# Fixing the issue order of SyncE and GpSimd and moving the bulk weight loads to the GpSimd queue, in a fused attention and mixer kernel

## The chip, the core and the metric

The kernel runs on one core of one Trainium2 chip. Its time is the device time of one execution in microseconds (us). Before the change the median of three runs was 1606.46 us (1606.43 to 1606.93).

The engines are called TensorE (PE in the profile; PEld are its weight loads), VectorE (DVE), ScalarE (ACT), GpSimd (POOL) and SyncE (SP). Sixteen DMA engines serve all DMA queues of the core. A DMA issued from SyncE goes to queue q1, which the profile calls hardware_dynamic; one issued from GpSimd goes to q0, software_dynamic.

## The reference, cut to what matters

```python
def reference(x, mem0, Wq, Wk, Wv, Wo, seg_len, _, w1, w2, w3, w4):    # S=2048, D=1024, H=32, Dh=128, F=3584
    xn = layernorm(x)
    return x + A(xn) + B(xn)

def A(xn):            # segments of 32 tokens, each behind 8 memory rows carried on from the segment before
    for s in range(64):
        h = concat([mem, xn[s*32:(s+1)*32]])
        q, k, v = h@Wq, h@Wk, h@Wv                  # 32 heads of 128
        p = softmax(mask(q @ k.T * scale))
        o = (p @ v) @ Wo
        mem, out[s] = o[:8], o[8:]

def B(xn):
    h  = gelu(layernorm(xn) @ w1)
    x1 = xn + shift_channels(h) @ w2                # four channel groups, shifted along S by 1, -1, 2, -2
    return x1 + gelu(layernorm(x1) @ w3) @ w4
```

Inputs and outputs are bf16. The kernel works through it in these stages, whose names are used below:

- **first phase**: layernorms of x, the transposed tile `xn2T`, `@ w1`, gelu;
- **second phase**: `@ w2` on the shifted channels, residual, layernorm, the transposed result `xn3T`;
- **MLP**: `@ w3`, gelu (`h3T`), `@ w4`. Small units for the memory rows are mixed in, each with a 1 MB tile of Wv or Wo (`wt`, `wot`);
- **V phase**: V = xn @ Wv, written to DRAM;
- **attention**: five blocks of tokens, each with eight head groups of four heads. A head group projects Q and K from `hTb`, the block's transposed tokens (64 matmuls of 396 columns, 403 in the first block; 128 matmuls in the last), and between those projections come scores (`psS`), softmax on VectorE and ScalarE (its result is `Pn`), a DMA transpose of `Pn` into `PT` (a DMA that transposes the tile as it copies it), and the output matmuls (`psO`) that read `PT` and `V`. After a block, `pso` multiplies its outputs by Wo.

One head group reads 1 MB of Wq, 1 MB of Wk and 0.4 MB of V. Each of its four score tiles needs one small transpose `Pn` to `PT`.

## The kernel before

TensorE alone was in a hand-written order (`manual_schedule`); the other engines' orders came from a scheduler. This is the part of the attention that matters. Cuts are marked.

```python
with tc.manual_schedule(engines={mybir.EngineType.PE}), ExitStack() as actx:
    wpool = actx.enter_context(tc.tile_pool(name="aw", bufs=4, side="right"))   # 4 weight tiles of 1 MB
    # ... first phase, second phase, MLP, V phase cut ...
    def load_values(B, V, hg):
        nc.sync.dma_start(V[0:96, 0:4, :], V_d[r:r + 384, cs_].rearrange("(t p) c -> p t c", p=96))
        # ... the memory rows of V, on nc.sync too; cut ...
    def scores(t, hg, QT, KTt):
        # ... 4 psS matmuls; mask, exp, sums, reciprocal on VectorE and ScalarE; cut ...
        nc.vector.tensor_tensor(Pn[:T, :, :T], e[:T, :, :T], rs[...], op=ALU.mult)   # ring of 3 Pn
        PT = smp.tile([P, 4, 112], BF16, tag="PT", bufs=5)
        nc.sync.dma_start_transpose(PTr, Pn[:rows].rearrange("p h k -> p (h k)"))
        return PTr

    def tick(us, blocked=None):          # a nominal clock: which scores (S) or outputs (O) go out now
        clock[0] += us
        while True:
            for i, (due, kind, fn) in enumerate(smalls):
                if due <= clock[0] and kind != blocked:
                    smalls.pop(i)
                    clock[0] += fn()
                    break
            else:
                return
    LAT = 8.0                            # outputs come due 8 us after their scores
    for gi_, group in enumerate(groups):
        for hg in range(8):
            wq, wk = wtile(), wtile()
            nc.sync.dma_start(wq[:], Wq_v[:, :, cs_])
            nc.sync.dma_start(wk[:], Wk_v[:, :, cs_])
            for B, V in zip(Bs, Vs):
                load_values(B, V, hg)
            if gi_ == 0 and hg < 4:
                nc.sync.dma_start(wo_sb[:, hg * 8:(hg + 1) * 8, :], Wo_v[:, hg * 8:(hg + 1) * 8, :])
            for w, dsts, scale in ((wq, QTs, QSCALE), (wk, KTs, None)):
                for hh in range(4):
                    proj(B, w, hh, dst, scale)
                    tick(...)
            # ... queue this head group's scores, due evenly over the next head group; cut ...
```

In the first phase four of 16 tiles of `xn2T` were transposed on TensorE, the others by DMA transposes on SyncE. `w2` (2 MB) was loaded after the third group. The second phase loaded `xn` and transposed `xn3T` on SyncE, tile by tile; `w3` (seven chunks of 1 MB) came behind it in the text, on SyncE too.

Of the kernel before, what the change touches and what calls it, by code (L numbers as in the profile page):

```python
# [23 lines left out]
P = 128  # L24
# [53 lines left out]
def kernel(  # L78
# [107 lines left out]
    with tc.manual_schedule(engines={mybir.EngineType.PE}), ExitStack() as actx:  # L186
# [5 lines left out]
        with ExitStack() as bctx:  # L192
            psum = bctx.enter_context(tc.tile_pool(name="psum", bufs=2, space=PSUM))
            with ExitStack() as hctx:
# [4 lines left out]
                nc.gpsimd.memset(hTB[:, :, 0:2], 0.0)  # L199
                nc.gpsimd.memset(hTB[:, :, S + 2:S + 4], 0.0)  # L200

                with ExitStack() as p0:
# [3 lines left out]
                    xts = [ring.tile([P, D], BF16, tag="xt", bufs=8, name=f"xt{n}") for n in range(NT)]  # L206

                    def load_x(n):
                        nc.sync.dma_start(xts[n][:], x_v[:, n, :])
# [5 lines left out]
                    for n in range(3, 8):  # L215
                        load_x(n)

                    def norm(n, xn2T, jj, on_pe):
                        xt = xts[n]
                        st = ring.tile([P, 2, 6], F32, tag="st")  # L220
                        for c in range(2):
                            nc.vector.bn_stats(st[:, c, :], xt[:, c * 512:(c + 1) * 512])
                        mv = ring.tile([P, 2], F32, tag="mv")
                        nc.vector.bn_aggr(mv[:], st[:])
                        ab = ring.tile([P, 2], F32, tag="ab")
                        nc.vector.tensor_scalar(ab[:, 0:1], mv[:, 1:2], EPS, None, op0=ALU.add)
                        nc.vector.tensor_scalar(ab[:, 1:2], ab[:, 0:1], EPS, mv[:, 1:2], op0=ALU.mult, op1=ALU.add)
                        rr = ring.tile([P, 2], F32, tag="rr")
                        nc.gpsimd.tensor_tensor(rr[:], ab[:], neghalf[:], op=ALU.pow)
                        nm2 = ring.tile([P, 1], F32, tag="nm2")  # L230
                        nc.vector.tensor_scalar(nm2[:], mv[:, 0:1], rr[:, 1:2], -1.0, op0=ALU.mult, op1=ALU.mult)
                        xn2 = ring.tile([P, D], BF16, tag="xn2")
                        nc.scalar.activation(xn2[:], xt[:], ACTF.Identity, bias=nm2[:], scale=rr[:, 1:2])
                        if not on_pe:
                            nc.sync.dma_start_transpose(xn2T[:, jj], xn2[:])
                        xn = ring.tile([P, D], BF16, tag="xn")
                        nc.vector.tensor_scalar(xn[:], xt[:], mv[:, 0:1], rr[:, 0:1], op0=ALU.subtract, op1=ALU.mult)
                        nc.gpsimd.dma_start(xn_v[:, n, :], xn[:])
                        if n + 8 < NT:
                            load_x(n + 8)  # L240
                        return xn, xn2

                    def transposes(xn2, xn2T, jj):
                        for k0 in (0, 4):
                            ps = psum0.tile([P, 4, P], F32, tag="tr")
                            for k in range(4):
                                nc.tensor.matmul(ps[:, k, :], xn2[:, (k0 + k) * P:(k0 + k + 1) * P], ident[:], start=True, stop=True)
                            if k0 == 0:
                                nc.vector.tensor_copy(xn2T[:, jj, k0:k0 + 4, :], ps[:])
                            else:  # L250
                                nc.scalar.copy(xn2T[:, jj, k0:k0 + 4, :], ps[:])
# [7 lines left out]
                    def stage1(n0, nt, xn2T, between):  # L259
                        w = nt * P  # L260
                        for co in range(KT):
# [5 lines left out]
                            if between and co % 2 == 1:  # L267
                                between.pop(0)()

                    groups = []  # L270
                    n0 = 0
                    for nt in (1, 1, 2, 2, 2, 4, 4):
                        groups.append((n0, nt))
                        n0 += nt
                    todo = []
                    prev = None
                    for (n0, nt) in groups:
                        xn2T = ring.tile([P, 4, KT, P], BF16, tag="xn2T", bufs=2)
                        on_pe = n0 < 4
                        trs, sms = [], []  # L280
                        for jj in range(nt):
                            xn, xn2 = norm(n0 + jj, xn2T, jj, on_pe)
                            if on_pe:
                                trs.append(lambda xn2=xn2, jj=jj, xn2T=xn2T: transposes(xn2, xn2T, jj))
                            sms.append(lambda n=n0 + jj, xn=xn: seg_sums(n, xn))
                        if prev is None:
                            for f in trs:
                                f()
                            todo = sms
                        else:  # L290
                            todo = trs + todo
                            stage1(*prev, todo)
                            for f in todo:
                                f()
                            todo = sms
                        prev = (n0, nt, xn2T)
                        if n0 == 4:
                            nc.sync.dma_start(w2_sb[:], w2_v)
                    stage1(*prev, todo)
                    for f in todo:  # L300
                        f()

# [34 lines left out]
            with ExitStack() as p3:  # L337
# [129 lines left out]
                while pending or units:  # L467
                    spec_step()
# [384 lines left out]
```

## Time and profile before

| stage (from the first and last TensorE instruction of each, in the trace) | us |
|---|---|
| first phase | 13.4 to 96.6 |
| second phase | 96.4 to 151.8 |
| MLP | 151.7 to 587.7 |
| V phase | 587.5 to 808.7 |
| attention | 809.6 to 1599.2 |
| span | 1604.6 |

From the page of the kernel before (span 1604.6 us): TensorE's busy time, its share and its instructions; and the DMA queues with packets, megabytes and the share of the 16 engines' time.

```profile
PE 1537.0 (96%) x10222; PEld 830.5 (52%) x10222; DVE 525.3 (33%) x1149; ACT 511.5 (32%) x1183; POOL 89.7 (6%) x114
...
q1 hardware_dynamic: 333888, 249.23, 58.2%
q0 software_dynamic: 6080, 21.05, 3.5%
```

TensorE is the limit: 96% busy. Nearly all bytes go through SyncE's queue. What is left to win stands in TensorE's waits of the kernel before: who waits, for what, the sum in us, how often, and the longest.

```profile
PE ps L247 <- ACT xn_152 L233: 13.4, 1, 13.4
PE psO L575 <- DMA PT<-Pn_6360: 10.1, 9, 2.1
PE ps L264 <- DMA xn2T<-xn_788: 8.2, 1, 8.2
PE ps L370 <- DMA wt<-in_A_Wv_dram: 5.2, 2, 3.9
PE ps L436 <- ACT h3T L437: 4.8, 1, 4.8
...
PE gps_3027 L384 <- DMA wot<-in_A_Wo_dram: 3.5, 2, 3.0
...
PE psO L575 <- DMA PT<-Pn_6359: 2.6, 3, 1.2
PE psO L575 <- DMA PT<-Pn_6361: 2.5, 4, 1.5
```

The start costs 13.4 us. The three PT lines together (one for each of the three Pn buffers) cost 15.2 us in the whole attention.

One more view: what SyncE issued in one head group of the kernel before, in order (start, us, instruction).

```profile
892.09 1.19 SPq L566 DMA_TRANSPOSE PT<-Pn_6361  x1
893.86 0.40 SPq L629 DMA_DIRECT2D wt<-in_A_Wq_dram  x1
895.12 1.19 SPq L566 DMA_TRANSPOSE PT<-Pn_6359  x1
896.41 1.47 SPq L524 DMA_DIRECT2D V_7498<-V_scratch  x1
898.26 1.18 SPq L566 DMA_TRANSPOSE PT<-Pn_6360  x1
...
900.41 0.57 SPq L630 DMA_DIRECT2D wt<-in_A_Wk_dram  x1
901.24 1.23 SPq L566 DMA_TRANSPOSE PT<-Pn_6361  x1
```

### The profile page before, as it was taken

How to read it: one execution, taken by the hardware profiler on the slowest of the kernel's cores; microseconds unless marked ns; L12 is line 12 of the kernel's file. 1: busy time of each engine (PE TensorE's matmuls, PEld its weight loads, DVE VectorE, ACT ScalarE, POOL GpSimd, SP SyncE). 2: the span in 40 equal slices, each digit the busy share in tenths (PEclk: the TensorE clock that was granted, in tenths of full speed). 3: DMA queues.
4: the chain of work that ended last, by engine and by line, in shares of the span. 5: the costliest groups of instructions: out<-in, count | busy, mean ns of one | idle time of the engine just before them, and what ended most of it. 6: DMA issues, size and time to landing. Idle time of an engine off the chain costs nothing.

```text
span 1604.6 us, 25081 instructions
## 1 busy us (share of the span) xinstructions
PE 1537.0 (96%) x10222; PEld 830.5 (52%) x10222; DVE 525.3 (33%) x1149; ACT 511.5 (32%) x1183; POOL 89.7 (6%) x114
## 2 busy tenths in 40 slices
PE   5799998999999999999999999999999999999998
PEld 4544444454454444444455645654655566466654
DVE  6248000001010112212235533551554165325541
ACT  4423300301202101111146623650563266146630
POOL 4223001001011010000000000000000000000000
PEclk9899999999999999999999999999999999999999
DMA  9869525265382567433369965993798388348521
GB/s 316 242 190 298 190 86 177 79 208 186 91 243 75 109 193 266 132 105 120 105 196 254 236 155 131 245 232 89 213 233 201 108 223 228 91 128 196 115 48 48
DMA packets 340087, 271.93 MB, mean 169 GB/s; under 512 B 155987, under 2 KB 309736, under 8 KB 339968
## 3 DMA queue, kind: packets, MB, share of 16 engines
q1 hardware_dynamic: 333888, 249.23, 58.2%
q0 software_dynamic: 6080, 21.05, 3.5%
q8 instruction: 82, 1.34, 0.4%
q14 instruction: 37, 0.30, 0.1%
HBM read 191.52 MB, written 42.53 MB: 146 GB/s over the span
## 4 chain that ended last, share of the span: by engine, by line
PE 73%; DMA 9%; DVE 1%; issue 1%; ACT 0%; POOL 0%; SPq 0%; ACTq 0%; POOLq 0%
PE ps L540 23%; PE pso L593 14%; PE ps L481 14%; PE ps L436 9%; PE ps L460 8%; DMA PT<-Pn_6360 3%; PE psO L575 2%; PE psS L551 2%; DMA PT<-Pn_6361 2%; DMA PT<-Pn_6359 1%; DMA hTb<-xn_scratch 1%; PE ps L693 1%; DMA R_scratch<-R_3128 1%; PE ps L404 1%; DMA wot<-in_A_Wo_dram 1%
## 5 line engine op out<-in xcount | busy, mean ns | idle before, releaser
L540 PE MATMUL ps<-hTb,wt 128*128 128x396 bf16 (+1 forms) x2560 | 403.7, 311 | 0.0
L540 PEld LDWEIGHTS <-wt 128*128 128x128 bf16 x3072 | 272.0, 98 | 167.3 <-issue 4.5
L481 PE MATMUL ps<-wt,xT 128*128 128x512 bf16 x1024 | 221.2, 379 | 0.0
L460 PE MATMUL ps<-w_sb,h3T 128*128 128x512 bf16 x896 | 198.5, 382 | 0.0
L437 ACT ACTIVATE h3T<-ps 128x512 bf16<-128x512 f32 x112 | 66.6, 597 | 315.0 <-PE ps L436 310.6
L481 PEld LDWEIGHTS <-xT 128*128 128x128 bf16 x1024 | 100.2, 98 | 120.8
L436 PEld LDWEIGHTS <-w_sb 128*128 128x128 bf16 x896 | 88.1, 99 | 112.3 <-issue 11.4
L460 PEld LDWEIGHTS <-h3T 128*128 128x128 bf16 x896 | 87.1, 98 | 103.3 <-issue 2.7
L557 DVE TENSOR_REDUCE sums<-sm 99x4 f32<-99x396 f32 (+1 forms) x176 | 97.6, 554 | 117.6 <-ACT sm L555 117.5
L553 DVE TENSOR_TENSOR sm<-psS,c_mask_reg_sb 99x396 f32<-99x396 f32 x160 | 91.2, 570 | 109.6 <-PE psS L551 108.9
L483 ACT CAST Vs<-ps 128x512 bf16<-128x512 f32 x64 | 37.4, 586 | 230.2 <-PE ps L481 177.5
L555 ACT ACTIVATE sm<-sm 99x396 f32<-99x396 f32 (+1 forms) x176 | 92.8, 527 | 54.0 <-DVE sm L553 49.8
L485 DVE CAST Vs<-ps 128x512 bf16<-128x512 f32 x64 | 44.3, 692 | 176.5 <-PE ps L481 172.7
L540 PE MATMUL ps<-hTb_5138,wt 128*128 128x403 bf16 x512 | 93.6, 335 | 2.4 <-ACT QT_6369 L544 1.5
L264 PE MATMUL ps<-xn2T,w_sb 128*128 128x256 bf16 (+2 forms) x448 | 65.9, 309 | 13.8 <-DMA xn2T<-xn_788 8.2
L601 DVE TENSOR_TENSOR ot<-pso,Rt 128x512 bf16<-128x512 f32 x32 | 22.1, 691 | 156.1 <-PE pso L593 152.8
L264 PEld LDWEIGHTS <-w_sb 128*128 128x128 bf16 x448 | 41.0, 106 | 32.7 <-issue 9.8
L436 PE MATMUL ps<-xn3T_1209,w_sb 128*128 128x512 bf16 x224 | 51.4, 393 | 4.8 <-ACT h3T L437 4.8
L315 PE MATMUL ps<-w_sb,hTB 128*128 128x512 bf16 x256 | 55.4, 379 | 0.0
L436 PE MATMUL ps<-xn3T_1210,w_sb 128*128 128x512 bf16 x224 | 51.0, 390 | 0.0
L436 PE MATMUL ps<-xn3T_1211,w_sb 128*128 128x512 bf16 x224 | 49.0, 379 | 0.0
L436 PE MATMUL ps<-xn3T_1212,w_sb 128*128 128x512 bf16 x224 | 48.5, 379 | 0.0
(613 smaller groups left out, 1407.1 us busy)
## 6 DMA issues: line engine op xcount, KB each, us to landing
wt<-in_A_Wq_dram SPq DMA_DIRECT2D x40, 1024.0 KB
wt<-in_A_Wk_dram SPq DMA_DIRECT2D x40, 1024.0 KB
wt<-in_A_Wv_dram SPq DMA_DIRECT2D x24, 1024.0 KB
w_sb<-in_B_w_dram SPq DMA_DIRECT2D x16, 1024.0 KB
V_scratch<-Vs SPq DMA_DIRECT2D x32, 512.0 KB
wot<-in_A_Wo_dram SPq DMA_DIRECT2D x8, 1024.0 KB
wo_sb<-in_A_Wo_dram SPq DMA_DIRECT2D x4, 2048.0 KB
Rt<-R_scratch SPq DMA_DIRECT2D x32, 256.0 KB
```

Source lines behind the costliest of these rows:

```text
L264: nc.tensor.matmul(ps[:, :w].rearrange("p (n t) -> p n t", t=P), w1_sb[:, k, co * P:(co + 1) * P], xn2T[:, :nt, k, :], start=(k == 0), sto ...
L315: nc.tensor.matmul(ps[:], hTB[:, k, o:o + P], w2_sb[:, k, ch * 512:(ch + 1) * 512], start=(k == 0), stop=(k == KT - 1))
L436: nc.tensor.matmul(ps[:].rearrange("p (n t) -> p n t", t=P), w3_sb[:, k, f * P:(f + 1) * P], xn3T[tb][:, :, k, :], start=(k == 0), stop=(k ...
L437: nc.scalar.activation(h3T[:, f, :], ps[:], ACTF.Gelu_apprx_tanh)
L460: nc.tensor.matmul(ps[:], h3T[:, f, j * P:(j + 1) * P], w4_sb[:, f, ch * 512:(ch + 1) * 512], start=(f == 0), stop=(f == FT - 1))
L481: nc.tensor.matmul(ps[:], xT[:, m4 * 4 + j, k, :], wv[:, k, :], start=(k == 0), stop=(k == KT - 1))
L485: nc.vector.tensor_copy(Vs[:, j, :], ps[:])
L540: nc.tensor.matmul(ps[:, :nb] if B["b"] in (0, 5) else ps[:, :nb].rearrange("p (t c) -> p t c", t=4), w[:, k, hh * P:(hh + 1) * P], B["rhs ...
L553: nc.vector.tensor_tensor(sm[:T, :, :T], S3, t["mask"][:].unsqueeze(1).to_broadcast((T, 4, T)), op=ALU.add)
L555: nc.scalar.activation(e[:T, :, :T], sm[:T, :, :T], ACTF.Exp, scale=LN2)
L557: nc.vector.tensor_reduce(ss, e[:T, :, :T], axis=AX.X, op=ALU.add)
L593: nc.tensor.matmul(self.ps[:], self.oX[:, h, self.gl * P:(self.gl + 1) * P], wo_sb[:, h, self.cc], start=(h == 0), stop=(h == H - 1))
```

## The change

Its intent: SyncE and GpSimd get a hand-written order too. Bulk weights go to GpSimd's queue, so that SyncE's queue is left to the transposes and small loads. The first phase is software-pipelined by hand, with VectorE and ScalarE in fixed order and eight of 16 tiles transposed on TensorE. Wo is loaded in the V phase instead of in the attention. The core of the diff (cuts marked):

```diff
-    with tc.manual_schedule(engines={mybir.EngineType.PE}), ExitStack() as actx:
+    with tc.manual_schedule(engines={mybir.EngineType.PE, mybir.EngineType.SP, mybir.EngineType.Pool}), ExitStack() as actx:
 # first phase (rewritten, cut): first xn2 on VectorE, groups of (1, 1, 2, 2, ...) tiles, NPE = 8 tiles transposed on TensorE
+            def load_w3(c):
+                nc.gpsimd.dma_start(w3_sb[:, :, c * 512:(c + 1) * 512], w3_v[:, :, c * 512:(c + 1) * 512])
+                        if n0 == 8:
                             nc.sync.dma_start(w2_sb[:], w2_v)
+                        if n0 >= 8:
+                            load_w3((n0 - 8) // 2)
 # second phase, tile n: xn loaded three tiles ahead
+                        load_xn(n + 3)
+                        nc.sync.dma_start_transpose(xn3T[n // 4][:, n % 4], xn3[:])
                         nc.gpsimd.dma_start(R1_v[:, n, :], x1[:])
-                        nc.sync.dma_start_transpose(xn3T[n // 4][:, n % 4], xn3[:])
+                        if n < 3:
+                            load_w3(4 + n)
-            for c in range(7):
-                nc.sync.dma_start(w3_sb[:, :, c * 512:(c + 1) * 512], w3_v[:, :, c * 512:(c + 1) * 512])
 # MLP: Wv and Wo tiles of the memory units on nc.gpsimd, asked for one or two units ahead (cut)
 # V phase: Wo here, Wv two head groups ahead
+                if 1 <= hg < 5:
+                    nc.gpsimd.dma_start(wo_sb[:, (hg - 1) * 8:hg * 8, :], Wo_v[:, (hg - 1) * 8:hg * 8, :])
 # attention
-                nc.sync.dma_start(V[0:96, 0:4, :], V_d[r:r + 384, cs_].rearrange("(t p) c -> p t c", p=96))
+                nc.gpsimd.dma_start(V[0:96, 0:4, :], V_d[r:r + 384, cs_].rearrange("(t p) c -> p t c", p=96))
 # (the memory rows of V likewise, cut)
-                nc.sync.dma_start(wq[:], Wq_v[:, :, cs_])
-                nc.sync.dma_start(wk[:], Wk_v[:, :, cs_])
+                nc.gpsimd.dma_start(wq[:], Wq_v[:, :, cs_])
+                nc.gpsimd.dma_start(wk[:], Wk_v[:, :, cs_])
         def tick(us, blocked=None):
             clock[0] += us
-            while True:
-                for i, (due, kind, fn) in enumerate(smalls):
-                    if due <= clock[0] and kind != blocked:
-                        smalls.pop(i)
-                        clock[0] += fn()
-                        break
-                else:
-                    return
+            done = set()                                  # one S and one O per step, at most five S without their O
+            for item in list(smalls):
+                due, kind, fn = item
+                if due <= clock[0] and kind != blocked and kind[0] not in done and not (kind[0] == "S" and flying[0] >= 5):
+                    smalls.remove(item)
+                    flying[0] += 1 if kind[0] == "S" else -1
+                    done.add(kind[0])
+                    clock[0] += fn()
```

## The prediction

> **What bounds the kernel now.** TensorE: the page gives it 1537.0 us busy of a 1604.6 us span, so 67.5 us idle. The list of waits names 61 of it: start 13.4; first phase, DMA transposes 8.2 and 3.6, a PSUM copy 1.8; weight loads in the MLP (speculative Wv and Wo tiles) 5.2 and 3.5; h3T after the second phase's last transpose 4.8; in the attention phase (after 800 us) the transposed probabilities PT 15.2, oT_m copies 2.9, others 2.4. Longer gaps cost twice: the clock records show half clock after those at 39, 60, 162, 264, 374 and 1415 us (16 matmuls of 512 columns took 6.50 us cold, 3.61 warm). Work ran in about 30 us of such stretches: 15 us lost. The Trainium skill ("TensorE: Matmul & The Clock Gate", Part 1) says that the gate halves the clock after an idle window of about 3.4 us; this trace agrees. So about 82 us can be won.
>
> **Step by step.**
> 1. Start. By hand, with the first xn2 on VectorE (0.54 us; on ScalarE 1.24 us, which waited until 12.09): x0 is there at 3.5, pow ends near 6.3, transposes near 7. Stage-1 matmuls start near 9 instead of 16.24. Gain 7.
> 2. First phase, rest. The waits 3.6 + 8.2 + 1.8 and about 4.5 of cold clock go. Added on TensorE: four more tiles transposed (about 2 us); 256-column matmuls at 119 ns for 512-column ones at 225, about +1.6. New danger: w2 (2 MB, over 6 us at the 316 GB/s seen) is issued on SyncE between the transposes of tiles 10 and 11, with a w3 chunk beside it: one stall of 3 to 5 us, then cold clock. The phase ended at 96.4; I expect 87 to 92: with step 1 a net gain of 7.
> 3. Second phase to MLP: h3T still waits for the last transpose (issued 158.5, landed 162.9): 0.
> 4. Speculative weights on the GpSimd queue, asked for a step (12 us or more) ahead, not behind SyncE's waits for R stores: 5.2 + 3.5 and two cold stretches of about 3 go. Gain 14.
> 5. V phase: 1024 matmuls without a wait in 221 us; Wo's 8 MB fits there (DMA share 0.3 to 0.8): 0.
> 6. Attention. SyncE issues each PT transpose in 1.19 us but also all loads, 0.3 to 1.5 each, and the DMA share is above 1.0 while Wo loads. On another queue these no longer precede PT. The Trainium skill ("DMA: Bandwidth & Descriptors", queues) says engines go round-robin between queues; no run here shows it yet. Score and output items also go out one of each kind per step. Of 20.5 us 6 stay: gain 14.
> 7. Tail (4.6 us): 0.
>
> Sum 35: **1571 us, range 1556 to 1594**. Faster by over 2%: 0.57; within 2%: 0.41; slower: 0.02.
>
> **What would show it.** Stage-1 matmuls from 9 us; first phase over by 92; a wait for xn2T at tile 10/11; none for wt or wot in the MLP; PT waits under 6 us in all; h3T gap unchanged; TensorE busy 1525 to 1533.
>
> **What would make it wrong.** Loads on the GpSimd queue slow to issue (1024 rows each) or blocked behind its in-order adds and stores; SyncE's fixed order holding PT behind the four hTb transposes or an out store; a larger w2 stall; or none and the h3T gap gone too, which would reach 1555.

## More of the kernel before

The next view, busy time by stage of the kernel before, has for each stretch its length, then busy us and instructions of PE, PEld, DVE, ACT and POOL, and last the granted TensorE clock, the DMA share and GB/s. The three lines are first phase, second phase and attention.

```profile
0.00:96.50 96.50, 69.29 (x609) 48.05 (x610) 40.85 (x133) 43.21 (x78) 26.07 (x45) 0.93 0.82 241
96.50:151.80 55.30, 55.30 (x260) 25.08 (x257) 46.10 (x102) 17.81 (x15) 20.12 (x30) 1.00 1.05 294
...
809.00:1604.00 795.00, 769.10 (x5764) 453.35 (x5764) 352.56 (x764) 343.92 (x913) 0.00 (x0) 1.00 0.68 169
```

The second phase has no idle TensorE time at all, although it moves 294 GB/s; the attention has 25.9 us of it (795.0 - 769.1).

In the whole attention, 95 of the 176 PT issues are followed by one bulk load (of Wq, Wk or the main part of V) before the next PT, 13 by more than one; in the kernel after it is 31 and 42.

## The result and the profile after

The changed kernel takes 1711.93 us (median of 4 runs, 1704.66 to 1727.47) against 1606.45 us (1605.87 to 1606.93) of the kernel before (the three runs above and one more): 1.067 times as long, 95% interval 1.059 to 1.075. Here and below a ratio is the mean time of one kernel's runs over the mean of the other's in the same rounds, so it is not quite the ratio of the medians quoted. The prediction had the direction wrong.

| stage | before, us | after, us | length changed by |
|---|---|---|---|
| start and first phase | ends 96.6 | 7.2 to 90.8 | -5.8 |
| second phase | 55.4 | 71.3 | +15.9 |
| MLP | 436.0 | 414.6 | -21.4 |
| V phase | 221.2 | 221.8 | +0.6 |
| attention | 789.6 | 911.0 | +121.4 |

Two gains came and one large loss swallowed them. From the page of the kernel after (span 1714.8 us), the lines that answer to those shown of before:

```profile
PE 1569.4 (92%) x10382; PEld 853.2 (50%) x10382; DVE 527.3 (31%) x1122; ACT 512.5 (30%) x1202; POOL 277.9 (16%) x381
...
q0 software_dynamic: 47728, 171.61, 34.4%
q1 hardware_dynamic: 187760, 97.64, 24.3%
```

171.6 MB now go through GpSimd's queue. TensorE's busy time grew by 32 us, though it does only 160 more matmuls. The view by stage of the kernel after (first phase, second phase, attention) shows why:

```profile
0.00:90.80 90.80, 69.31 (x769) 61.19 (x770) 42.96 (x122) 43.81 (x97) 32.67 (x57) 0.92 0.74 210
90.80:162.00 71.20, 60.59 (x258) 26.33 (x256) 46.97 (x93) 17.72 (x15) 23.31 (x48) 0.90 0.99 257
...
798.50:1714.00 915.50, 804.99 (x5764) 464.55 (x5764) 353.84 (x770) 344.93 (x913) 142.25 (x198) 0.95 0.63 150
```

In the attention the same 5764 matmuls took 805.0 us instead of 769.1, at a granted clock of 0.95 instead of 1.00. So of the loss of about 121 us, 36 are colder clock (805.0 - 769.1) and 85 are idle time ((915.5 - 805.0) - (795.0 - 769.1)). The colder clock is a consequence: the trace shows 19 stretches of half clock within the attention, each right after pauses of TensorE. The Trainium skill ("TensorE: Matmul & The Clock Gate", Part 1) puts the gate's idle window at about 3.4 us. The traces agree only in part: nine of the 19 stretches follow a pause of 3.6 us or more, but ten follow pauses of which the longest was 1.9 to 3.5 us, while other pauses of up to 2.2 us were followed by none. In the kernel before, the half clock at 374 us came after a pause of 3.0 us, and the one at 1415 us after pauses of at most 1.0 us. The gaps are the cause, then. TensorE's waits of the kernel after name them:

```profile
PE psO L652 <- DMA PT<-Pn_5177: 37.0, 16, 6.3
PE psO L652 <- DMA PT<-Pn_5176: 27.5, 11, 9.0
PE psO L652 <- DMA PT<-Pn_5178: 26.1, 15, 3.0
PE psS L628 <- DVE sm L630: 12.0, 3, 6.0
PE ps L287 <- DMA xn2T<-xn_943: 11.7, 1, 11.7
PE ps L270 <- DMA c_ident_sb<-c_ident: 7.2, 1, 7.2
PE ps L377 <- DVE x_1586 L378: 6.3, 1, 6.3
PE ps L377 <- DVE x_1624 L378: 4.4, 1, 4.4
PE ps L503 <- ACT h3T L504: 1.1, 1, 1.1
```

PT: 90.6 us instead of 15.2. The transposes that were to have the SyncE queue to themselves became the largest wait of the kernel. The waits for `wt` and `wot` in the MLP are gone, as predicted, and the start is 7.2 instead of 13.4.

Was PT issued late, or did it land late? What GpSimd and SyncE issued around two head groups of the kernel after:

```profile
1054.81 0.70 POOL L601 DMA_DIRECT2D V_9149<-V_scratch  x1 [6.58 <-PE psS L628]
1055.50 0.57 POOL L606 DMA_DIRECT2D V_9149<-Vmem_scratch  x1
1056.07 0.93 POOL L707 DMA_DIRECT2D wt<-in_A_Wq_dram  x1
1059.42 0.89 POOL L708 DMA_DIRECT2D wt<-in_A_Wk_dram  x1 [2.43 <-PE ps L617]
1069.99 0.70 POOL L601 DMA_DIRECT2D V_9322<-V_scratch  x1 [9.69 <-PE psS L628]
```

```profile
1054.05 1.19 SPq L643 DMA_TRANSPOSE PT<-Pn_5177  x1
1057.41 1.19 SPq L643 DMA_TRANSPOSE PT<-Pn_5178  x1
1060.30 1.22 SPq L643 DMA_TRANSPOSE PT<-Pn_5176  x1
1063.56 1.19 SPq L643 DMA_TRANSPOSE PT<-Pn_5177  x1
```

SyncE is free: in this stretch it issues nothing but PT, in about 1.2 us each. GpSimd hands out the 2.4 MB of a head group within 5 us (1054.81 to 1059.42), as soon as buffers come free, and then nothing for 10 us. So the DMA engines get a burst, and three PT transposes fall into it. The DMA packet records show what it does to them. A PT is 448 packets of 256 bytes (192 for eight of them in the last block), 28 on each of the 16 DMA engines if they are spread evenly, and its packets can be told apart by size and order. I put the 176 PT of each kernel in classes by the bytes of all other packets that started between a PT's issue and its last packet (256-byte packets, which are those of transposes, left out). In the table are the number of PT, the median us from issue to last packet, and the median us from first to last packet (classes between are left out):

| other MB moved meanwhile | before | after |
|---|---|---|
| under 0.05 | 34 PT, 1.89, 0.71 | 56 PT, 1.88, 0.71 |
| 0.8 to 1.2 | 68 PT, 4.57, 1.19 | 40 PT, 5.40, 1.62 |
| 1.2 to 1.8 | 9 PT in this row and the next, 5.63 to 5.91 | 34 PT, 7.59, 2.66 |
| over 1.8 | | 12 PT, 9.92, 4.85 |

A PT alone takes 1.9 us in both kernels. Beside more than 1.8 MB it takes 9.9 us (at most 11.8), which is more than the 8 us (`LAT`) that the hand-written order leaves between scores and outputs. Before, no PT took longer than 6.4 us. About half of the delay comes before PT's first packet: with over 1.8 MB beside it that started 5.0 us after the issue (median), alone 1.2 us. The table alone proves no cause, since a PT that is late for any reason sees more bytes go by; the experiments below have to show it.

I also split each wait for PT of over 0.3 us by what was late. "Softmax" means that Pn was written over 4 us after the start of its last score matmul, "issue" that SyncE issued the PT over 1 us after Pn was written. "Transfer" is the rest: softmax and issue were on time.

| kernel | waits, us | of it transfer | softmax | issue | mean issue to last packet in the transfer class |
|---|---|---|---|---|---|
| before | 17.9 | 10.9 | 4.9 | 2.2 | 5.1 us |
| after | 90.4 | 71.7 | 12.4 | 6.3 | 7.7 us |

(The sums differ a little from the wait lists, as gaps are counted from the end of the matmul before. The 17.9 us also hold four waits, 2.7 us in all, whose PT had landed over 35 us earlier; the wait list puts such waits down to the copy into `oT_m`.) Four fifths of the time is transfers that were issued at once and landed late. Part of the rest is the same thing at one remove: VectorE's copies of the next block's `hTb` wait for DMA transposes of their own, and the softmax stands behind them. From VectorE's waits in the attention of the kernel after (13.8 us in the kernel before for the first line, 3.2 for the second, whose load of the residual tile `Rt` the change also asks for at an earlier place):

```profile
DVE hTb L593 <- DMA hTb<-xn_scratch: 46.8, 15, 8.4
DVE ot L677 <- DMA Rt<-R_scratch: 23.0, 5, 6.8
```

The second phase lost its 16 us in a like way. SyncE in the kernel after, while three chunks of w3 (3 MB) went out on GpSimd's queue at 99.3, 101.8 and 104.7:

```profile
101.44 0.52 SPq L366 DMA_DIRECT2D xn_1504<-xn_scratch  x1
102.48 10.49 SPq L391 DMA_TRANSPOSE xn3T_1418<-xn_1502  x1
...
113.65 8.67 SPq L391 DMA_TRANSPOSE xn3T_1418<-xn_1541  x1
```

Issuing one transpose held SyncE for 10.49 us, and the next for 8.67; before, the same issue took 1.2 to 2.9 us. The `xn` loads are behind them in SyncE's fixed order, VectorE waits for those, and TensorE's two pauses of 6.3 and 4.4 us follow (the two `x` lines of the wait list). The 11.7 us at `xn2T` in the first phase has the same face: SyncE was held for 11.07 us from 48.64 by one transpose, behind `w2` and beside a w3 chunk.

### The profile page after: what moved, and what is told of

The parts are those of the page before. It is cut to its first block, busy times and chain, and to the rows that moved or that the text cites. A ratio compares the mean times of both kernels' runs of the same rounds, so it can differ in the third digit from the quotient of the medians.

```text
span 1714.8 us, 25420 instructions
## 1 busy us (share of the span) xinstructions
PE 1569.4 (92%) x10382; PEld 853.2 (50%) x10382; DVE 527.3 (31%) x1122; ACT 512.5 (30%) x1202; POOL 277.9 (16%) x381
## 4 chain that ended last, share of the span: by engine, by line
PE 47%; DMA 17%; SPq 1%; DVE 1%; issue 0%; ACT 0%; POOL 0%; ACTq 0%; POOLq 0%; DVEq 0%
PE ps L617 18%; PE pso L671 13%; PE ps L561 12%; DMA PT<-Pn_5178 6%; DMA PT<-Pn_5176 5%; DMA PT<-Pn_5177 3%; DMA hTb<-xn_scratch 2%; PE psO L652 2%; PE psS L628 1%; SPq L592 1%; PE ps L771 1%; DMA wt<-in_A_Wq_dram 0%; DMA R_scratch<-R_5095 0%; DMA V_scratch<-Vs 0%; DVE ot L677 0%
## 5 line engine op out<-in xcount | busy, mean ns | idle before, releaser
L617 PE MATMUL ps<-hTb,wt 128*128 128x396 bf16 (+1 forms) x2560 | 431.4, 324 | 1.5 <-ACT QT_8460 L621 0.6
L617 PEld LDWEIGHTS <-wt 128*128 128x128 bf16 x3072 | 283.1, 101 | 185.8 <-issue 34.6
L561 PEld LDWEIGHTS <-xT 128*128 128x128 bf16 x1024 | 100.2, 98 | 121.4 <-issue 0.7
L503 PEld LDWEIGHTS <-w_sb 128*128 128x128 bf16 x896 | 86.8, 98 | 104.0 <-issue 1.4
L563 ACT CAST Vs<-ps 128x512 bf16<-128x512 f32 x64 | 37.4, 586 | 233.8 <-PE ps L561 176.4
L617 PE MATMUL ps<-hTb_5354,wt 128*128 128x403 bf16 x512 | 98.5, 346 | 1.7 <-DVE Vs L565 0.9
L708 POOL DMA_DIRECT2D wt<-in_A_Wk_dram x40 | 35.6, 890 | 282.5 <-PE psO L652 137.7
L287 PE MATMUL ps<-xn2T,w_sb 128*128 128x256 bf16 (+1 forms) x576 | 65.2, 272 | 13.2 <-DMA xn2T<-xn_943 11.7
L377 PE MATMUL ps<-w_sb,hTB 128*128 128x512 bf16 x256 | 60.7, 402 | 10.6 <-DVE x_1586 L378 6.3
L287 PEld LDWEIGHTS <-w_sb 128*128 128x128 bf16 x576 | 52.7, 103 | 19.7 <-issue 14.0
L503 PE MATMUL ps<-xn3T_1418,w_sb 128*128 128x512 bf16 x224 | 48.8, 379 | 1.1 <-ACT h3T L504 1.1
L503 PE MATMUL ps<-xn3T_1421,w_sb 128*128 128x512 bf16 x224 | 49.0, 379 | 0.0
L503 PE MATMUL ps<-xn3T_1420,w_sb 128*128 128x512 bf16 x224 | 49.0, 379 | 0.0
```

What stands on the lines that cost most here:

```text
L287: nc.tensor.matmul(ps[:, :w].rearrange("p (n t) -> p n t", t=P), w1_sb[:, k, co * P:(co + 1) * P], xn2T[:, :nt, k, :], start=(k == 0), sto ...
L377: nc.tensor.matmul(ps[:], hTB[:, k, o:o + P], w2_sb[:, k, ch * 512:(ch + 1) * 512], start=(k == 0), stop=(k == KT - 1))
L503: nc.tensor.matmul(ps[:].rearrange("p (n t) -> p n t", t=P), w3_sb[:, k, f * P:(f + 1) * P], xn3T[tb][:, :, k, :], start=(k == 0), stop=(k ...
L561: nc.tensor.matmul(ps[:], xT[:, m4 * 4 + j, k, :], wv[:, k, :], start=(k == 0), stop=(k == KT - 1))
L617: nc.tensor.matmul(ps[:, :nb] if B["b"] in (0, 5) else ps[:, :nb].rearrange("p (t c) -> p t c", t=4), w[:, k, hh * P:(hh + 1) * P], B["rhs ...
```

## The experiments

**Theory A**: the attention is slower because the bulk loads moved to GpSimd's queue, and share the DMA engines with PT there. **Rival B**: the new step rule (one S and one O per step, at most five in flight) delays the small items. **Rival C**: SyncE's fixed order holds PT behind other things. B was tested on the kernel before only.

### e1_attn_hw: the attention loads back on SyncE, fixed order kept

```diff
+            def load_qk(hg):                                # called one head group ahead
+                qk.append((wtile(), wtile()))
+                nc.sync.dma_start(qk[-1][0][:], Wq_v[:, :, c_])
+                nc.sync.dma_start(qk[-1][1][:], Wk_v[:, :, c_])
-                nc.gpsimd.dma_start(V[0:96, 0:4, :], V_d[r:r + 384, cs_]...)      # and the other V loads
+                nc.sync.dma_start(V[0:96, 0:4, :], V_d[r:r + 384, cs_]...)
-                nc.gpsimd.dma_start(wq[:], Wq_v[:, :, cs_])
-                nc.gpsimd.dma_start(wk[:], Wk_v[:, :, cs_])
+                wq, wk = qk.pop(0)                          # all of V, Wq, Wk at the start of a head group
```

> The changed kernel with one thing undone: in the attention phase the loads of Wq, Wk and V go back to the SyncE queue (Wq and Wk asked for one head group ahead in program order); the fixed order, the new step rule and all earlier phases stay. Theory A (weight loads on the GpSimd queue move in 4096-byte packets of about 190 ns, and a DMA engine alternates them with the 256-byte, 18 ns packets of a PT transpose, so PT lands late): the tail of PT issue to last packet (95th percentile 9.3 us, max 11.8 in the changed kernel) falls to 6.5 us or less, TensorE's waits for PT fall from 90 us to under 25, the attention phase from 911 us to under 815, the time to about 1605 to 1625. Rival B (the new one-of-each-kind-per-step rule) and rival C (SyncE's fixed order) both leave it above 1680.

Measured: 1722.34 us (1719.60 to 1727.54), ratio 1.073 (1.070 to 1.076). Theory A's number fell: the queue alone was not it. But C was not shown either. Of 110.2 us of PT waits, 74.9 were issue, 33.9 transfer. SyncE's own order shows what happened (from the trace of this run):

```profile
1047.65 0.53 SPq L611 DMA_DIRECT2D V<-V_scratch  x1
...
1048.64 0.40 SPq L554 DMA_DIRECT2D wt<-in_A_Wq_dram  x1
1049.14 0.52 SPq L555 DMA_DIRECT2D wt<-in_A_Wk_dram  x1
1049.76 4.40 SPq L653 DMA_TRANSPOSE PT<-Pn  x1
```

My edit had put the 2.4 MB of a head group in one burst as well, now ahead of PT in the same queue. The first PT issue behind this burst held SyncE for 4.40 us instead of 1.19; in the whole run the longest took 5.6 us, and 48 of the 176 PT were issued over 1 us after their Pn was written (2 in the changed kernel). So the theory was changed to **A2**: what counts is how many bulk bytes are handed out between a PT's issue and its landing. The queue is second.

### e3_before_pool: the kernel before, with the attention's Wq, Wk and V on GpSimd

```diff
-                nc.sync.dma_start(wq[:], Wq_v[:, :, cs_])
-                nc.sync.dma_start(wk[:], Wk_v[:, :, cs_])
+                nc.gpsimd.dma_start(wq[:], Wq_v[:, :, cs_])
+                nc.gpsimd.dma_start(wk[:], Wk_v[:, :, cs_])
 # and all V loads; scheduler's order and old step rule as before
```

> The kernel before with one part of the change alone: Wq, Wk and V of the attention phase are loaded through the GpSimd queue; old step rule, no fixed order on SyncE or GpSimd. Theory A: PT waits rise from 15 us to over 60, attention from 790 us to over 850, the time to 1660 to 1720; the packets of queue 0 are of 4096 bytes. Rivals B and C: within 10 us of 1606.

Measured: 1672.64 us (1651.81 to 1675.91), ratio 1.037 (1.030 to 1.045). The attention took 848 us, PT waits 53.9 us. That is a little under theory A's numbers for the attention (850) and the waits (60). Moving the loads is enough to lose by itself, without fixed order on SyncE and without the new step rule. It is about half of the loss.

### e2_before_tick: the kernel before, with the new step rule only

```diff
-            while True:
-                for i, (due, kind, fn) in enumerate(smalls): ...
+            done = set()
+            for item in list(smalls): ...                   # the rule of the change, word for word
```

> The kernel before with the new step rule alone (one score and one output item per step, at most five in flight). Rival B: over 1660 us, with PT waits above 60 us. Theory A: within 12 us of 1606, either way.

Measured: 1593.61 us (1592.29 to 1597.34), ratio 0.992 (0.989 to 0.995). On the kernel before B is refuted: the rule is a small gain. (In the changed kernel, e6 and e8 below keep the rule, and the loss is gone there.)

### e4_pad and e11_halves: the size of a packet

The packet records show packets of 4096 bytes on GpSimd's queue, a median of 188 ns each in the attention, and of 1024 bytes at 46 ns on SyncE's. A PT packet that takes turns with larger ones would wait longer for each turn. Two edits tried to shrink them.

```diff
-            return wpool.tile([P, KT, 512], BF16, tag="w", name="wt")                       # e4_pad
+            return wpool.tile([P, KT, 520], BF16, tag="w", name="wt")[:, :, 0:512]
-                nc.gpsimd.dma_start(wq[:], Wq_v[:, :, cs_])                                 # e11_halves, wk likewise
+                for c in range(2):
+                    nc.gpsimd.dma_start(w_[:, :, c * 256:(c + 1) * 256], W[:, :, hg * 512 + c * 256:hg * 512 + (c + 1) * 256])
```

> The changed kernel with padded weight tiles: each of the 8 rows of 512 in a partition now sits in a row of 520, so a partition's 8 KB are no longer contiguous in SBUF. If the GpSimd queue's 4096-byte packets come of joining rows that are contiguous in SBUF, they become 1024-byte packets here, and by theory A (an alternation packet by packet) a PT packet then waits for 46 to 60 ns and not for 190: PT's 95th percentile falls under 7 us, PT waits from 90 us to under 45, the time to under 1660. If packets stay at 4096 bytes, nothing changes (1700 to 1730) and the run says nothing of theory A. If packets become 1024 bytes and the time stays above 1690, it is not the packet's size but the second queue as such.

> The changed kernel with each attention load of Wq and Wk split into two column halves on the same GpSimd queue: rows of 512 bytes. If the queue joins four rows to a packet, its packets become 2048 bytes and half as long, and if a DMA engine alternates packet by packet, the spread from a PT's first to its last packet under load (median 4.9 us with over 1.8 MB moved) falls to about 2.5 to 3.5 us, PT waits from 90 to under 65 us. If packets stay at 4096 bytes the spread stays. Short rows may also slow the loads themselves: the time is not forecast beyond 1650 to 1740.

Measured: e4_pad 1706.91 us (1702.75 to 1717.39), ratio 1.064 (1.060 to 1.069); e11_halves 1752.36 us (1746.87 to 1761.32), ratio 1.091 (1.088 to 1.095). In both, the packets of GpSimd's queue stayed at 4096 bytes (medians of 185 and 226 ns). So both are inconclusive for the question they were made for. Rows half as long were slower still (PT waits 132 us).

### e8_no_loads: Wq and Wk loaded once only

```diff
-                nc.gpsimd.dma_start(wq[:], Wq_v[:, :, cs_])
-                nc.gpsimd.dma_start(wk[:], Wk_v[:, :, cs_])
+                if gi_ == 0 and hg == 0:
+                    wq, wk = wtile(), wtile()
+                    nc.gpsimd.dma_start(wq[:], Wq_v[:, :, cs_])
+                    nc.gpsimd.dma_start(wk[:], Wk_v[:, :, cs_])
```

This computes wrong attention weights. (The comparison with the reference at these magnitudes does not see which weights made Q and K.)

> Wrong result on purpose: the changed kernel, but Wq and Wk of the attention phase are loaded once and reused, so 78 of the 80 loads of 1 MB are gone; V loads, fixed order and step rule stay. Theory A2 (PT lands late in proportion to the bulk bytes that move between its issue and its landing, whatever the queue): PT waits fall from 90 us to under 8, attention from 911 us to under 780, the time to under 1590. Rival C (SyncE's fixed order) or E (VectorE's and ScalarE's new order) keeps attention above 860 us.

Measured: 1579.78 us (1576.65 to 1583.81), ratio 0.984 (0.979 to 0.990). Attention 773 us, PT waits 2.4 us, median issue to last packet 1.88 us. Fixed order, step rule and transposes are all still there; only the bytes are gone, and the loss is gone with them. This settles C: the order of SyncE is not the cause. It also gives the floor: with nothing to disturb PT, most head groups take 12.3 us.

### e5_pool_paced and e6_sp_paced: the same loads one at a time, on either queue

Wq of the next head group goes out after the first Q projection, V after the fourth, Wk after the second K projection. In e5 GpSimd issues them, each held back by a small copy that reads the projection just written; in e6 SyncE issues them at the same places in its order.

```diff
+                def between(is_q, hh, dst):
+                    at = (is_q, hh)
+                    if at not in ((True, 0), (True, 3), (False, 1)):
+                        return
+                    nc.gpsimd.tensor_copy(pace[0:1, 0:1], dst[0:1, hh, 0:1])   # e5 only
+                    if at == (True, 3):
+                        for B, V in zip(Bs, Vs):
+                            load_values(B, V, hg)                              # nc.gpsimd in e5, nc.sync in e6
+                    elif more:
+                        load_qk((hg + 1) % 8, Wq_v if is_q else Wk_v)          # one load each
```

> The changed kernel with the same loads on the same GpSimd queue, but handed out one by one: GpSimd waits (by copying one element of a Q or K tile) for the head group's 1st Q, 4th Q and 2nd K projection before it issues Wq of the next group, V, and Wk of the next group, instead of all 2.4 MB within 5 us. Theory A2 (bursts): the share of PTs with over 1.2 MB moved before they land falls from 46 of 176 to under 15, PT waits from 90 us to under 40, attention to under 840 us, the time to 1610 to 1650; the queue of itself costs some tens of us as in e3 (attention 848 us). Rival A (the second queue as such is what hurts): time above 1680.

> As e5, at the same places, but issued on SyncE in its fixed order, between the PT transposes. Theory A2: attention under 800 us (e2, the kernel before with the new step rule, has 783), PT waits under 20 us, time 1585 to 1610. Rival C (the fixed order on SyncE itself): attention above 850 us as in e1 (911).

Measured: e5 1648.70 us (1632.85 to 1651.42), ratio 1.023 (1.016 to 1.031), attention 845 us, PT waits 56.6. e6 1595.76 us (1591.33 to 1602.36), ratio 0.993 (0.987 to 0.998), attention 791 us, PT waits 4.4. So e5 missed two of its numbers (PT waits under 40 us, attention under 840). In e6 a new wait came up, since Wq and Wk were asked for only about 7 us (median) before they were needed: 9.8 and 4.8 us. With e1 and the changed kernel this makes a square of the attention's length (one profiled execution each; the changed kernel's four runs alone span 23 us):

| attention, us | on GpSimd's queue | on SyncE's queue |
|---|---|---|
| all loads of a head group in one burst | 911 (after) | 912 (e1) |
| one load at a time | 845 (e5) | 791 (e6) |

A burst is as bad on either queue. Taking it apart is worth 66 us on GpSimd and 121 on SyncE. And with the burst gone, the choice of queue makes a difference of 54 us.

### e7_w3_spread: w3 spread over the first two phases

```diff
-                        if n0 == 8:
+                        if n0 == 2:
                             nc.sync.dma_start(w2_sb[:], w2_v)
-                        if n0 >= 8:
-                            load_w3((n0 - 8) // 2)
+                        if n0 in (1, 2, 4):
+                            load_w3({1: 0, 2: 1, 4: 2}[n0])
-                        if n < 3:
-                            load_w3(4 + n)
+                        if n in (1, 4, 7, 10):
+                            load_w3(3 + n // 3)
```

> The changed kernel with w2 issued at the third group of the first phase and w3's seven chunks moved off the transposes: three during tiles 1 to 5, four in the second phase at tiles 1, 4, 7, 10 instead of three at tiles 0 to 2. Theory A2: the 11.7 us wait for xn2T and its cold clock go (the first phase ends at 76 to 81 us instead of 91), the second phase falls from 71 us to 55 to 59, the rest does not move: 25 us less than the changed kernel, 1680 to 1695. If the second phase stays at 65 us or more, w3's chunks are not what held SyncE there.

Measured: 1728.87 us (1720.50 to 1741.64), ratio 1.078 (1.070 to 1.086). A miss. The first phase gained (it ends at 85.3, the stall at `xn2T` is gone), but the second phase took 86.5 us instead of 71. Even chunks one at a time held SyncE's transposes there: five issues of over 4 us, the longest 11.2. That stage already moved 294 GB/s before the change, and there is no good place in it for w3 on another queue.

### e10_lat12: the outputs come due 12 us after their scores instead of 8

```diff
-        LAT = 8.0
+        LAT = 12.0
```

> The changed kernel with one number changed: output items are placed 12 us (model time) behind their scores and not 8. Theory A2 says that the loss is PT's latency beyond the 8 us that the order allows, not throughput: PT waits fall from 90 us to under 45, though Pn's three buffers and the limit of five in flight may turn some of it into waits of the scores (psS) for VectorE; time 1640 to 1690. If the DMA engines simply could not carry the traffic, nothing would be gained: 1700 or more.

Measured: 1648.76 us (1646.20 to 1652.55), ratio 1.029 (1.025 to 1.032). Attention 837 us, PT waits 29.6 us instead of 90.6, though a PT takes no less time from issue to last packet than in the changed kernel (median 4.76 us against 3.78, 95th percentile 9.57 against 9.33). The bytes fit well enough into the time; it is PT's lateness against its deadline that costs. Some of the gain went to other waits (Wq 14.8 us, KT 5.1).

### e9_both: both losses taken away

From what the runs pointed to: the attention's loads on SyncE, one at a time, asked for earlier than in e6 (Wq of the next head group at the start of this one, Wk after the third Q projection, V after the first K projection); and w3 out of the second phase. For that all 16 tiles of `xn2T` are transposed on TensorE, so that the first phase has no DMA transposes, and w2 and all of w3 are loaded there.

```diff
-                    NPE = 8
+                    NPE = NT
-                        if n0 == 8:
+                        if n0 == 2:
                             nc.sync.dma_start(w2_sb[:], w2_v)
-                        if n0 >= 8:
-                            load_w3((n0 - 8) // 2)
+                        if n0 >= 2:
+                            load_w3((n0 - 2) // 2)
-                        if n < 3:
-                            load_w3(4 + n)
+                if more:
+                    load_qk((hg + 1) % 8, Wq_v)                     # nc.sync
+                def between(is_q, hh):
+                    if (is_q, hh) == (True, 2) and more:
+                        load_qk((hg + 1) % 8, Wk_v)
+                    elif (is_q, hh) == (False, 0):
+                        for B, V in zip(Bs, Vs):
+                            load_values(B, V, hg)                   # nc.sync
```

> A version meant to beat both: the changed kernel, with the attention loads on SyncE one at a time (Wq of the next head group at its start, Wk after the 3rd Q projection, V after the 1st K projection), all 16 tiles of the first phase transposed on TensorE (8 more, 0.55 us each), w2 at the third group and one w3 chunk per group from there on, none in the second phase. By theory A2: the first phase ends at 80 to 84 us (91 in the changed kernel), the second phase takes 55 to 57 us (71), attention 773 to 790 us (911; e6 had 791, with 15 us of waits for Wq and Wk that come from asking too late), the time 1560 to 1580. If the second phase stays near 70 us, w3's chunks were not its cause; if the first phase still waits for xn2T or x, not w2 but something else held it.

Measured: 1560.65 us (six runs, 1557.51 to 1564.86) against 1604.75, ratio 0.973 (0.971 to 0.976): faster than both kernels. The first phase ends at 82.0 us, the second takes 55.4, the MLP 415, the attention 777. From the page and TensorE's waits of this run:

```profile
PE 1522.7 (98%) x10372; PEld 843.8 (54%) x10446; DVE 532.0 (34%) x1130; ACT 508.5 (33%) x1210; POOL 132.1 (8%) x173
```

```profile
PE psO L659 <- DMA PT<-Pn: 10.2, 9, 3.5
PE ps L270 <- DMA c_ident_sb<-c_ident: 6.8, 1, 6.8
...
PE ps L501 <- ACT h3T L502: 1.7, 1, 1.7
```

TensorE is busy 98% of the span. The intent of the change holds in the first phase and the MLP; it was the attention's loads and the second phase's w3 chunks that were in the wrong place.

### e12_pool_same and e13_act: the same places as e9, from another queue

These two were to ask what the queue itself costs when bytes and places are the same. In e12 GpSimd issues the attention's loads where e9 has them, each held back by a copy that reads the newest Pn. In e13 ScalarE issues them, on a second hardware queue of its own.

```diff
-                nc.sync.dma_start(qk[-1][0][:], W[:, :, hg * 512:(hg + 1) * 512])      # e9; V loads likewise
+                nc.gpsimd.tensor_copy(pace[0:1, 0:1], pns[(pn_at[0] - 1) % 3][0:1, 0, 0:1])   # e12
+                nc.gpsimd.dma_start(qk[-1][0][:], W[:, :, hg * 512:(hg + 1) * 512])           # e12
+                nc.scalar.dma_start(qk[-1][0][:], W[:, :, hg * 512:(hg + 1) * 512])           # e13
```

> e9_both with one thing changed: the attention loads go to the GpSimd queue again, at the same places; before each, GpSimd copies one element of the newest Pn tile, so that it issues just when SyncE has issued the transpose of that tile, as SyncE did in e9. If the software queue itself costs (e5 against e6: 54 us, but the loads were not issued at the same times there), attention rises from 777 to 800 us or more, and PT's spread from first to last packet with 0.8 to 1.2 MB moved rises from 1.1 us to 1.6 us or more. If only bursts and timing matter, attention stays within 10 us of 777 and the time within 12 us of 1561.

> e9_both with the attention loads issued from ScalarE, a second hardware queue. Packets of 1024 bytes (46 to 60 ns) from the other queue, so if engines alternate packet by packet a PT's 28 packets per engine wait for about 1.5 us more at worst, against some 5 us beside the 4096-byte packets of the software queue: PT's spread with over 0.8 MB moved stays under 2.5 us in the median; attention 775 to 815 us. ScalarE's issue time (0.3 to 0.6 us a load, near 150 loads) and its waits for tiles may cost 10 to 30 us of that. If attention is over 840, any second queue hurts, not only the software one.

Measured: e12 1600.31 us (1594.30 to 1601.63), ratio 0.997 (0.993 to 1.000), attention 815. e13 1655.14 us (1645.45 to 1664.07), ratio 1.034 (1.029 to 1.038), attention 864. The split of the PT waits, made as before:

| kernel | waits, us | transfer | softmax | issue | median last data packet to matmul in these waits | PT with a late completion, of 176 | VectorE's wait for `hTb` |
|---|---|---|---|---|---|---|---|
| e6, SyncE | 4.4 | 1.9 | 0.4 | 2.2 | 0.71 | 6 | 10.3 |
| e5, GpSimd | 56.4 | 38.9 | 13.9 | 3.6 | 4.69 | 37 | 39.7 |
| e9, SyncE | 9.9 | 1.3 | 4.8 | 3.8 | 0.71 | 5 | 11.5 |
| e12, GpSimd | 37.4 | 19.8 | 14.0 | 3.5 | 2.75 | 30 | 28.2 |
| e13, ScalarE | 68.0 | 3.4 | 64.6 | 0.0 | 0.91 | 32 | 41.5 |

e12 is 38 us longer in the attention than e9 (815 - 777). The difference lies in the tail: the median from issue to last packet is not longer (2.73 us, e9 3.23), the 95th percentile is (6.15, e9 5.09). And the last data packet is not yet the landing. In these traces a DMA tells of its landing by 16 increments of a semaphore, and in e12's waits the matmul started a median of 0.05 us after the last of them. The column "late completion" counts the PT for which that increment came over 2 us after the last data packet. For PT with 0.8 to 1.2 MB beside them, first to last packet took 1.45 us against 1.08; I had expected at least 1.6, so this sign of packets taking turns came out weaker than expected. VectorE waited longer for `hTb`, though the `hTb` transposes themselves were not slower from issue to landing (median 3.5 us, e9 4.9).

But e12 did not hit e9's places exactly, so it does not isolate the queue. Its loads went out a median of 0.61 us after SyncE began to issue the PT before them, while that issue was still going on; in e9 it was 1.28 us, since SyncE has to end the issue (1.2 us) first. Of e12's 30 late completions, 27 are of PT with a bulk load issued from 0.3 us before to 0.9 us after the start of their own issue; of the 58 PT with none from 1.5 us before to 1.2 us after, one was late. It is the same with 31 of the 37 in e5 and 28 of the 32 in e13, and in e6 and e9 no load was issued in that stretch. So what a second queue costs may be the moment of issue, which SyncE's own order rules out, and not GpSimd's queue as such. No run tests that.

e13 missed its expectation for a reason of its own. PT's data packets were like e9's (95th percentile 5.47 us), though 32 completions were late. But ScalarE, which computes the softmax's exponentials, now issues the loads as well, and Pn came a median of 4.40 us after the start of its last score matmul instead of 2.87. So this run doesn't say what a second hardware queue costs by itself; it says that ScalarE is the wrong engine to issue bulk loads from here.

## Why the prediction was wrong, point by point

- **Step 1, start: right.** Predicted 7 us, with stage-1 matmuls from 9; they start at 8.45 instead of 16.24.
- **Step 2, first phase: right at its end, a term mis-sized.** 90.8, in the predicted 87 to 92. The stall at tiles 10 and 11 was 11.7 us, not 3 to 5.
- **Step 3, second phase to MLP, "0": wrong.** I looked only at the h3T gap, which became 1.1 us in this profile (1 to 7 us in other runs). I costed w3's last three chunks at nothing, and the second phase grew by 16 us. With them out of it, the second phase took 55.4 us again (e9). Spreading them inside that phase didn't help (e7).
- **Step 4, weights in the MLP: mechanism right, size under-estimated.** Predicted 14; the MLP gained 21.4, some of it from the smaller h3T gap, which step 3 had held fixed. No waits for `wt` or `wot` are left.
- **Step 5, V phase: right** (221.2 and 221.8 us with Wo's 8 MB in it).
- **Step 6, attention: the step that failed.** It read: "On another queue these no longer precede PT. The Trainium skill ('DMA: Bandwidth & Descriptors', queues) says engines go round-robin between queues", and from it "gain 14". The runs showed a loss of 121, and PT waits of 90.6 us where they were to stay under 6. It is true that PT no longer queued behind loads on SyncE. But it still shares the DMA engines with them, and what delays PT is bulk handed out in a burst around its issue, on whatever queue (911 us on GpSimd's, 912 on SyncE's): it took 1.9 us with no bulk beside it, 9.9 us beside more than 1.8 MB. The kernel before had them spread out, one load between each two PT. An in-order queue on an engine with nothing else to do hands them out as soon as buffers come free, 2.4 MB in 5 us. I had that trace of before in front of me, and saw the loads between the PT issues as a cost to remove, not as pacing.
- **Sizes of the parts.** Burst: about 66 us of the 121 (after against e5; that also asks a head group ahead, so it is pace and place together). GpSimd's queue, together with the moments of issue that came with it: 38 us (e12 against e9) to 54 us (e5 against e6). What was left of e6 against e9, 14 us, is the places. Of the loss, 36 us came as colder clock after the gaps.
- **The step rule, "one of each kind per step": right in sign** (e2, 0.992).
- **Of the named dangers**, a larger w2 stall came true, and "SyncE's fixed order holding PT" did not (e8). The first, "loads on the GpSimd queue slow to issue or blocked", was the reverse of what happened: they were issued too freely.

**What stays open**: whether GpSimd's queue delays PT more than SyncE's when its loads are issued at the same moments (e12's were not), and why completions come late when a load is issued together with a PT. Taking turns packet by packet with 4096-byte packets would fit a part of the delay: with over 1.8 MB beside it, a PT's 28 packets per engine took 4.85 us, 173 ns each, about one such packet (188 ns), against 0.71 us, 25 ns each, alone. But the packet size could not be changed (e4, e11), at 0.8 to 1.2 MB the effect was weaker than that (e12), and the other half of the delay comes before PT's first packet. It is argued, not shown.

## What to carry to other kernels

A queue of its own gave the small urgent transfers no priority here: count the bulk bytes that will be handed out between the urgent transfer's issue and its deadline, and put one bulk load at a time between them, ideally in the same ordered queue, where no load can go out while the urgent transfer is being issued. When you move loads to an idle engine, ask what will hold them back there; if it is only free buffers, they will come in bursts. And bulk that must come early belongs in a stage without DMA transposes; to make such a stage, transposing on TensorE cost little here (e9).

## What the Trainium skill lacked or had wrong

- "DMA: Bandwidth & Descriptors", "Issuing engines are not separate DMA queues", says that DMAs from all issuers interleave on the same 16 engines, and that several issuers only save issue time. The runs agree with the first half, and I should have read it against my step 6. It lacks the other side: a cheaper issue can cost. The attention went from 790 to 911 us when loads that had paced themselves in SyncE's order were issued freely from GpSimd.
- The same page, "Queues, rings and completion order", says engines go round-robin between queues, a whole packet at a time. No run here shows the turns themselves. The page gives no latency for a small transfer beside bulk. Here: 448 packets of 256 bytes, 1.9 us alone, 5.4 us beside about 1 MB and 9.9 us beside more than 1.8 MB (at most 11.8).
- It gives a packet as about 9 to 17 descriptors, and elsewhere as preferably at most 4096 bytes. The packet records here count bytes and not descriptors. They fit the second: 4096 bytes on the software queue for rows of 1024 and of 512 bytes, padded or not (medians of 185 to 226 ns). What the page lacks is that the same weights went in packets of 1024 bytes (46 ns) on a hardware queue.
- The same page, "Rules for kernel authors", says "A transpose next to ordinary DMAs needs nothing". That is about correctness, where the runs agree (every run passed its comparison). For time it misleads: next to three 1 MB loads, issuing one transpose held SyncE for 10.49 us, and with it every load behind it.
- No page that I read says that issuing bulk loads from ScalarE delays its activations: Pn came 4.40 instead of 2.87 us after its scores (e13).
- "TensorE: Matmul & The Clock Gate", Part 1, gives an idle window of about 3.4 us. In the attention of the kernel after, ten of 19 stretches of half clock followed pauses of which the longest was 1.9 to 3.5 us.
